# Two tokens across the partitions in the gate scatter of an expert layer: one L for a pair of tokens, an R with zeros, two products per pair, five row buffers

## Chip, cores and metric

The kernel runs on one core of a Trainium2 chip. The metric is device time in microseconds of one execution. The kernel before takes 1112.83 us, the median of three runs (1112.5 to 1113.57). A profiled execution, taken separately, has its own time.

## What is computed

The output is the sum of three things over 2048 tokens of 512 values: the input, a Fourier mixing of its layer norm (matrix products with given DFT matrices), and a product-key expert layer (PEER). The last is what the change touches:

```python
q = einsum("nd,dhc->nhc", xf, w_q)              # 32 heads
s1, s2 = q1 @ k1.T, q2 @ k2.T                   # 64 + 64 key scores per head
# the best two of each, their four sums, the best two of those:
top_s, top_e = ...                              # per token 32 heads x 2 experts out of 4096
g   = softmax(top_s, axis=-1)
act = gelu(einsum("nd,nhkd->nhk", xf, u[top_e]))
out = einsum("nhk,nhk,nhkd->nd", g, act, v[top_e])
```

Each token so has 64 entries, each an expert number and a gate.

## The kernel before

**Stages.** First comes a stage of some 440 us: layer norm, the Fourier part and, in 8 chunks of heads by 16 blocks of 128 tokens, the scores (`scores`, L793) and the choice of experts (`routing`, L630), whose lists go into `z`. Then comes the expert stage, on which the change bears. It does not gather rows of `u` and `v` for most tokens, but multiplies densely with all 4096 experts. For a block `b` of 128 tokens:

- `u_part(b, cg)` (L950), eight parts: 48 products of 128x128x128 per part give the scores of 512 experts (L959), and ScalarE evicts them through the gelu into `act` (L962).
- `g_mm(b, tg)` (L974), four groups of 32 tokens: makes the dense gate matrix G (4096 experts by 32 tokens) by products of one-hot matrices. An expert number is split as `e = 128*c + l`. For one token, `L[entry, l]` is 1 where `l` is the entry's low part and `R[entry, c]` is the gate where `c` is its high part; L transposed times R is that token's 128x32 table of gates. VectorE makes L by an equality (L983) and R by an equality and a product (L991, L994) from the compacted lists `cmp`; TensorE makes one 128x32 product per token (L996) into a PSUM tile `pg` of two banks, of which there are two.
- `w_part(b, tg)` (L1002): VectorE multiplies the table with the activations, in place in PSUM (L1007); ScalarE writes the float16 high half (L1012) and VectorE the rest (L1015), both into `act`. L1015 is the last reader of the `pg` tile.
- `v_part(b, pv, cg)` (L1019), eight parts of 12 products 128x128x512 (L1024), and `finish` (L1037).

**The entries.** A gate is kept as two float16 halves. Before the change the two halves are two entries with the same expert, so that a token has 128 entries, one in each partition: `z` has the rows low part, high part and gate, each of 2 experts x 2 halves x 32 heads. `compact` (L693) transposes the three rows of a block (L698) and copies them to `cmp` with each value doubled (L699).

**The last two blocks** (256 tokens, `NS`) go another way: `fetch` (L1046) gathers, with an indirect DMA issued by GpSimd, one row of `[u|v]` for each of 128 token partitions into one of `BUFS` = 6 row buffers (tag `ga`); `dot` (L1054) takes the product with x on VectorE (L1066); `gain` (L1069) scales the row on ScalarE (L1076, L1077, L1079); GpSimd adds it (L1084) and then issues the next fetch. There are 128 such rows. `paced` and `pick` spread these and a series of checks of the inputs (`cx`, `fit`) over the parts.

**The order.** The parts alternate: `v_part` of block b with `g_mm(b+1, 2)` after part 3 and `g_mm(b+1, 3)` after part 7, then `u_part` of block b+2 with `g_mm(b+2, 0)` and `g_mm(b+2, 1)` at the same places. A scheduler sets the final order on each engine; each engine then works strictly in its order, and semaphores make it wait.

L has two buffers and a group uses both, one for each 16 tokens; R has two buffers and a group uses one.

Of the kernel before, what the change touches and what calls it, by code (L numbers as in the profile page):

```python
# [10 lines left out]
F16 = mybir.dt.float16  # L11
# [4 lines left out]
AF = mybir.ActivationFunctionType  # L16
ALU = mybir.AluOpType
AX = mybir.AxisListType

P = 128  # L20
# [3 lines left out]
NT = S // P  # L24
H = 32
# [3 lines left out]
NC = E // P  # L29
# [7 lines left out]
def tile_fnet_peer(ctx, tc, x, ca, cb, c5, wt, wf, wr, wq, kt, ut, vn, uv, out):  # L37
# [14 lines left out]
    z_d = dram.tile([NT, P, 3 * P], F16, name="z_d")  # L52
# [189 lines left out]
    cmp_p = stE.enter_context(tc.tile_pool(name="cmpp", bufs=1, side="right"))  # L242
# [313 lines left out]
    def part_b(safe, stS, stP, stE, xt, u_sb, cmp_p):  # L556
# [54 lines left out]
        sp = stS2.enter_context(tc.tile_pool(name="sp", bufs=1, side="left"))  # L611
        z = sp.tile([P, NT, 3, 2, 2, H], F16, name="z")
# [17 lines left out]
        def routing(part, j, vals, idx, t0=0, t1=NT, ge=nc.gpsimd):  # L630
# [6 lines left out]
            hs = slice(j * HC, (j + 1) * HC)  # L637
            n = t1 - t0
            idx = idx[:, t0:t1]
            zi = z[:, t0:t1]  # L640
            c00, c01, c10, pm, i2s = t("c00"), t("c01"), t("c10"), t("pm"), t("i2s")
            if part == 0:
                a = vals[:, t0:t1, 0].rearrange("p i k h -> p i h k")
                b = vals[:, t0:t1, 1].rearrange("p i k h -> p i h k")
# [6 lines left out]
            elif part == 1:  # L651
                ex, g = c10, sp.tile([P, n, 2, HC], F32, tag="g", name=f"g{j}_{t0}", bufs=1)
# [4 lines left out]
                nc.vector.tensor_copy(zi[:, :, 2, :, 0, hs], g)  # L657
                if not safe and t1 == NT:
                    nc.gpsimd.tensor_copy(gts[:, :, :, hs], g[:, n - NS:])
                nc.vector.tensor_tensor(zi[:, :, 2, :, 1, hs], g, zi[:, :, 2, :, 0, hs], op=ALU.subtract)  # L660
            else:
# [31 lines left out]
        def compact(b, src, pool, tag):  # L693

            cmp = pool.tile([P, 3, P, 2], F16, tag=tag, name=f"cmp{b}")
            p = pc(f"zt{b}", F16) if b < 2 else psum.tile([P, 512], F16, tag="pb", name=f"zt{b}", bufs=2)
            for w in range(3):
                nc.tensor.transpose(p[:, w * P:(w + 1) * P], src[:, w], ident16)  # L698
            nc.scalar.activation(cmp, p[:, :3 * P].rearrange("p (w n) -> p w n", w=3).unsqueeze(3)  # L699
                                 .to_broadcast([P, 3, P, 2]), AF.Copy)  # L700
            CMP[b] = cmp
# [163 lines left out]
        for j in range(NCH):  # L865
# [8 lines left out]
            for i in range(NT):  # L874
# [20 lines left out]
                if j + 1 == NCH and i == NT - 1:  # L895
                    for b in range(2):
                        compact(b, z[:, b].rearrange("p w k t h -> p w (k t h)"), cmp_p, f"cmp{b}")
                    nc.sync.dma_start(z_d[2:4].rearrange("i p f -> p i f"),
                                      z[:, 2:4].rearrange("p i a k t h -> p i (a k t h)"))
# [6 lines left out]
        for part in range(3):  # L906
            routing(part, *pend, 4, NT, nc.vector)
        nc.sync.dma_start(z_d[4:].rearrange("i p f -> p i f"),
                          z[:, 4:].rearrange("p i a k t h -> p i (a k t h)"))
# [7 lines left out]
        RS = [lr.tile([P, 32, NC], F16, name=f"R{k}") for k in range(2)]  # L917
# [16 lines left out]
        BUFS = 6  # L934
# [10 lines left out]
        def compact_d(b):  # L945
            zb = bp.tile([P, 3, P], F16, tag="zb", name=f"zb{b}", bufs=1)
            nc.sync.dma_start(zb.rearrange("p a r -> p (a r)"), z_d[b])
            compact(b, zb, cmp_p, f"cmp{b % 2}")
# [25 lines left out]
        def g_mm(b, tg, after=None):  # L974
            cmp = CMP[b]
            p = pg(f"g{b}_{tg}")
            def bc(w, t0, t1, n):
                return cmp[:, w, tg * TG + t0:tg * TG + t1, :].unsqueeze(2).to_broadcast([P, t1 - t0, n // 2, 2])

            for hf in range(2):  # L980
                LS.append(LS.pop(0))
                L = LS[-1]
                nc.vector.tensor_tensor(  # L983
                    L.rearrange("p t (l two) -> p t l two", two=2),
                    io_lam.rearrange("p (l two) -> p l two", two=2).unsqueeze(1).to_broadcast([P, 16, P // 2, 2]),
                    bc(0, hf * 16, hf * 16 + 16, P), op=ALU.is_equal)
                if hf == 0:
                    RS.append(RS.pop(0))
                    R = RS[-1]
                    Rv = R.rearrange("p t (c two) -> p t c two", two=2)  # L990
                    nc.vector.tensor_tensor(  # L991
                        Rv, io_c.rearrange("p (c two) -> p c two", two=2).unsqueeze(1)
                        .to_broadcast([P, TG, NC // 2, 2]), bc(1, 0, TG, NC), op=ALU.is_equal)
                    nc.vector.tensor_tensor(Rv, Rv, bc(2, 0, TG, NC), op=ALU.mult)  # L994
                for t in range(16):
                    i = nc.tensor.matmul(p[:, hf, t * NC:(t + 1) * NC], L[:, t, :], R[:, hf * 16 + t, :],  # L996
                                         start=True, stop=True)
# [495 lines left out]
```

## Time and profile before

| | |
|---|---|
| time, median of three runs | 1112.83 us |
| the profiled execution: its time | 1110.31 us |
| its span, first to last instruction | 1108.5 us |
| mean granted TensorE clock | 0.988 |
| PE busy (matmul) | 1070.5 us, 97% |
| DVE (VectorE) busy | 963.9 us, 87% |
| ACT (ScalarE) busy | 717.3 us, 65% |
| POOL (GpSimd) busy | 595.4 us, 54% |
| DMA moved | 196.78 MB, 178 GB/s |

PE is TensorE's matmul row, PEld its loads of weights. In a row of the timeline the first number is the start in us, the second the busy time; `[...]` at its end is idle time ahead of it and what ended that. Matmuls overlap: the time between two starts is what one costs, and is less than the duration of one. "x" counts instructions.

### The profile page before, as it was taken

The numbers are of one execution on the slowest core, as the hardware profiler recorded it, in microseconds if no ns is written. First come the engines' busy times: TensorE is split into PE (matmuls) and PEld (weight loads), VectorE is DVE, ScalarE is ACT, GpSimd is POOL, SyncE is SP. The second block draws the span as 40 slices with busy tenths as digits, with TensorE's granted clock in tenths as the row PEclk, the third lists the DMA queues.
The fourth block names the chain that finished last, engine by engine and source line by source line (L and its number), as shares of the span: only waits on it lengthen the run. The fifth ranks groups of instructions, "written<-read, shape, count | busy, mean of one in ns | idle before, by whom it ended". The sixth has DMA issues, their size and how long they took to land. (4 is left out here: it accounts for less than half of the span.)

```text
span 1108.5 us, 28483 instructions
## 1 busy us (share of the span) xinstructions
PE 1070.5 (97%) x11070; PEld 696.6 (63%) x11070; DVE 963.9 (87%) x2748; ACT 717.3 (65%) x1326; POOL 595.4 (54%) x553
## 2 busy tenths in 40 slices
PE   5899999999999999999989999999999999999987
PEld 4355555454544544987675967858667696776933
DVE  6879897979999999987999798999998889998971
ACT  3566657778788767533756766668666776767650
POOL 0013537588797846211646575665575656556431
PEclk9799999999999999999999999999999999999999
DMA  8248153435445331463568667766876667666511
GB/s 326 84 168 288 39 210 99 174 130 208 152 153 197 110 123 65 152 212 92 183 189 248 193 206 244 223 220 191 242 232 214 209 204 252 222 200 200 166 29 51
DMA packets 84936, 196.78 MB, mean 178 GB/s; under 512 B 10770, under 2 KB 27559, under 8 KB 84792
## 3 DMA queue, kind: packets, MB, share of 16 engines
q1 hardware_dynamic: 63898, 123.55, 33.0%
q0 software_dynamic: 20736, 71.31, 21.7%
q8 instruction: 88, 1.44, 0.5%
q14 instruction: 56, 0.46, 0.1%
q10 hardware_dynamic: 158, 0.01, 0.0%
HBM read 177.74 MB, written 17.10 MB: 176 GB/s over the span
## 5 line engine op out<-in xcount | busy, mean ns | idle before, releaser
L799 PE MATMUL s<-m,xq 128*128 128x512 f16 x1536 | 338.9, 379 | 0.0
L959 PE MATMUL z<-xb,u 128*128 128x128 f16 x5376 | 306.4, 220 | 0.0
L959 PEld LDWEIGHTS <-u 128*128 128x128 f16 x5376 | 302.1, 98 | 0.0
L1024 PE MATMUL v<-v,act 128*128 128x512 f16 x1344 | 300.2, 382 | 1.6 <-DVE act L1015 1.6
L1084 POOL TENSOR_TENSOR ov<-ov,ga 128x512 f32<-128x512 f32 x128 | 176.9, 1382 | 206.9 <-ACT ga L1079 173.4
L799 PEld LDWEIGHTS <-xq 128*128 128x128 f16 x1536 | 148.3, 98 | 171.3 <-issue 0.2
L1024 PEld LDWEIGHTS <-act 128*128 128x128 f16 x1344 | 129.6, 98 | 153.2 <-issue 4.5
L983 DVE TENSOR_TENSOR L<-io_lam,cmp 128x2048 f16<-128x2048 f16 x112 | 154.7, 1405 | 31.2 <-PE g L996 31.1
L1050 POOL DMA_INDIRECT ga<-in_uv_dram,eix x128 | 153.4, 1198 | 48.1 <-POOL ov L1084 36.9
L807 DVE MAX8 vals<-ss 128x8 f32<-128x64 f32 x1024 | 152.5, 216 | 14.0 <-ACT ss L804 14.0
L962 ACT ACTIVATE act<-z,scl 128x512 f32<-128x512 f32 x112 | 76.1, 681 | 93.6 <-PE z L959 92.9
L811 DVE FIND_INDEX8 idx<-vals,ss 128x8 uint16<-128x256 f32 x256 | 107.1, 419 | 0.0
L804 ACT ACTIVATE ss<-s,wsc 128x512 f32<-128x512 f32 x112 | 75.5, 680 | 43.1 <-PE s L799 33.8
L1079 ACT ACTIVATE ga<-ga,za 128x512 f32<-128x512 f32 x128 | 92.3, 722 | 10.2 <-ACT za L1077 0.4
L781 ACT ACTIVATE cx<-cx 128x896 f32<-128x896 f32 x64 | 60.6, 947 | 48.7 <-DVE cx L761 36.3
L1066 DVE SCALAR_TENSOR_TENSOR ga<-ga,px 128x512 f32<-128x512 f32 x128 | 85.7, 676 | 0.2
L1012 ACT ACTIVATE act<-g 128x1024 f16<-128x1024 f32 x56 | 73.2, 1308 | 18.2 <-DVE g L1007 18.2
L1007 DVE SCALAR_TENSOR_TENSOR g<-act,scl,g 128x1024 f32<-128x1024 f32 x56 | 71.6, 1279 | 10.7 <-ACT act L962 6.6
L1015 DVE TENSOR_TENSOR act<-g,act 128x1024 f16<-128x1024 f32 x56 | 72.7, 1298 | 6.6 <-ACT act L1012 6.5
L169 POOL TENSOR_TENSOR wq<-wq,wh 128x1024 f16<-128x1024 f32 x26 | 55.5, 2136 | 24.2 <-ACT wq L166 23.7
L996 PE MATMUL g<-R,L 128*128 128x32 f16 x1792 | 53.8, 176 | 13.0 <-DVE act L1015 12.5
L996 PEld LDWEIGHTS <-L 128*128 128x128 f16 x1792 | 51.6, 96 | 21.7 <-DVE act L1015 8.7
(281 smaller groups left out, 1298.4 us busy)
## 6 DMA issues: line engine op xcount, KB each, us to landing
cx<-in_cb_dram SPq DMA_DIRECT2D x50, 448.0 KB
wq<-in_wq_dram SPq DMA_DIRECT2D x32, 512.0 KB
fit<-in_wq_dram SPq DMA_DIRECT2D x28, 512.0 KB
uv<-in_ut_dram SPq DMA_DIRECT2D x16, 512.0 KB
uv<-in_vn_dram SPq DMA_DIRECT2D x16, 512.0 KB
cx<-in_cb_dram SPq DMA_DIRECT2D x28, 224.0 KB
xq<-in_x_dram SPq DMA_DIRECT2D x8, 512.0 KB
xt_d<-xq SPq DMA_DIRECT2D x16, 256.0 KB
```

What stands on the lines that cost most here:

```text
L799: mm = nc.tensor.matmul(ps, xt[i][:, l, kd, :], m[:, r, kd, :], start=(n == 0), stop=(n == 3 * KD - 1))
L807: nc.vector.max(vals[:, i, w, :, h], s[:, g, :])
L811: nc.vector.max_index(idx[:, i, w].rearrange("p k h -> p (k h)"), vals[:, i, w, 0:2].rearrange("p k h -> p (k h)"), s[:, w * HC:g + 1, :]. ...
L959: mm = nc.tensor.matmul(p[:, cc * P:(cc + 1) * P], ug[:, l, c % 2, kd, :], xb[:, r, kd, :], start=(n == 0), stop=(n == 3 * KD - 1))
L962: GL[mm.ins.name] = nc.scalar.activation(act[:, cg * 4:cg * 4 + 4, :].rearrange("p c n -> p (c n)"), p, AF.Gelu_apprx_tanh, scale=zsc)
L983: nc.vector.tensor_tensor(L.rearrange("p t (l two) -> p t l two", two=2), io_lam.rearrange("p (l two) -> p l two", two=2).unsqueeze(1).to_ ...
L996: i = nc.tensor.matmul(p[:, hf, t * NC:(t + 1) * NC], L[:, t, :], R[:, hf * 16 + t, :], start=True, stop=True)
L1024: mm = nc.tensor.matmul(pv, w16[:, c, :, l], vg[:, r, c % 2, :], start=(c == 0 and k == 0), stop=(c == NC - 1 and k == 2))
L1050: nc.gpsimd.indirect_dma_start(out=t, out_offset=None, in_=uv, in_offset=bass.IndirectOffsetOnAxis(ap=eix[:, n].rearrange("p k h -> p (k h ...
L1066: nc.vector.scalar_tensor_tensor(t, t, 1.0, T["x"], op0=ALU.mult, op1=ALU.mult, accum_out=T["z", n][:, s:s + 1])
L1079: nc.scalar.activation(t, t, AF.Copy, scale=z)
L1084: T["a"] = nc.gpsimd.tensor_tensor(o, o, t, op=ALU.add)
```

## The change

The two halves of a gate are no longer two entries. `z` has five rows of 64 entries: low part, high part, gate high half, gate low half, and the low part once more. `compact` transposes two neighbouring rows at a time, four transposes, so that partitions 0 to 63 get one row and 64 to 127 the next; three copies then put the entries of even tokens in partitions 0 to 63 and those of odd tokens in 64 to 127 of `cmp`, now `[128, 4, 64 pairs, 2]`.

In `g_mm` one L of 16 x 128 columns serves the 16 pairs of a group. R has, for each half of the gate and each pair, 64 columns: 32 for the even token, filled in partitions 0 to 63, and 32 for the odd one, filled in partitions 64 to 127. The other quarters stay zero; GpSimd zeroes both R once. VectorE makes a one-hot matrix for the high parts once and multiplies it with the gates in four pieces of 64 partitions. A pair takes two products of 128x64, for the two halves of the gate, which add up in PSUM, both with the same L. There are so still 32 products in a group.

R takes twice the space, and there is a tile `one_hot`; `BUFS` goes from 6 to 5.

```diff
-    z = sp.tile([P, NT, 3, 2, 2, H], F16, name="z")
+    z = sp.tile([P, NT, 5, 2, H], F16, name="z")
...
-                for l in range(2):
-                    for w, v in enumerate((lc, e)):
-                        ge.tensor_copy(zi[:, :, w, :, l, hs], v)
+                for w, v in ((0, lc), (1, e), (4, lc)):
+                    ge.tensor_copy(zi[:, :, w, :, hs], v)
...
-            cmp = pool.tile([P, 3, P, 2], F16, tag=tag, name=f"cmp{b}")
+            cmp = pool.tile([P, 4, 64, 2], F16, tag=tag, name=f"cmp{b}")
...
-            for w in range(3):
-                nc.tensor.transpose(p[:, w * P:(w + 1) * P], src[:, w], ident16)
-            nc.scalar.activation(cmp, p[:, :3 * P].rearrange("p (w n) -> p w n", w=3).unsqueeze(3)
-                                 .to_broadcast([P, 3, P, 2]), AF.Copy)
+            for w in range(4):
+                nc.tensor.transpose(p[:, w * P:(w + 1) * P], src[:, w:w + 2].rearrange("p w s -> p (w s)"), ident16)
+            for a, w0, w1, o in ((0, 0, 4, 0), (1, 0, 3, 1), (1, 3, 4, -3)):
+                r = slice(64 * a, 64 * a + 64)
+                nc.scalar.activation(cmp[r, w0 + o:w1 + o], p.rearrange("p (w n a) -> p w a n", w=4, a=2)[r, w0:w1, a]
+                                     .unsqueeze(3).to_broadcast([64, w1 - w0, 64, 2]), AF.Copy)
...
-        RS = [lr.tile([P, 32, NC], F16, name=f"R{k}") for k in range(2)]
+        RS = [lr.tile([P, 2, 16, 2, NC], F16, name=f"R{k}") for k in range(2)]
+        one_hot = lr.tile([P, 16, NC], F16, name="one_hot")
+        for R in RS:
+            nc.gpsimd.memset(R, 0.0)
...
-        BUFS = 6
+        BUFS = 5
...
-            for hf in range(2):
-                LS.append(LS.pop(0))
-                L = LS[-1]
-                nc.vector.tensor_tensor(
-                    L.rearrange("p t (l two) -> p t l two", two=2),
-                    io_lam.rearrange("p (l two) -> p l two", two=2).unsqueeze(1).to_broadcast([P, 16, P // 2, 2]),
-                    bc(0, hf * 16, hf * 16 + 16, P), op=ALU.is_equal)
-                if hf == 0:
-                    RS.append(RS.pop(0))
-                    R = RS[-1]
-                    Rv = R.rearrange("p t (c two) -> p t c two", two=2)
-                    nc.vector.tensor_tensor(
-                        Rv, io_c.rearrange("p (c two) -> p c two", two=2).unsqueeze(1)
-                        .to_broadcast([P, TG, NC // 2, 2]), bc(1, 0, TG, NC), op=ALU.is_equal)
-                    nc.vector.tensor_tensor(Rv, Rv, bc(2, 0, TG, NC), op=ALU.mult)
-                for t in range(16):
-                    i = nc.tensor.matmul(p[:, hf, t * NC:(t + 1) * NC], L[:, t, :], R[:, hf * 16 + t, :],
-                                         start=True, stop=True)
+            LS.append(LS.pop(0))
+            RS.append(RS.pop(0))
+            L, R = LS[-1], RS[-1]
+            nc.vector.tensor_tensor(
+                two(L), io_lam.rearrange("p (l two) -> p l two", two=2).unsqueeze(1).to_broadcast([P, 16, P // 2, 2]),
+                bc(0, P), op=ALU.is_equal)
+            nc.vector.tensor_tensor(
+                two(one_hot), io_c.rearrange("p (c two) -> p c two", two=2).unsqueeze(1)
+                .to_broadcast([P, 16, NC // 2, 2]), bc(1, NC), op=ALU.is_equal)
+            for l in range(2):
+                for a in range(2):
+                    r = slice(64 * a, 64 * a + 64)
+                    nc.vector.tensor_tensor(two(R[r, l, :, a]), two(one_hot[r]), bc(2 + l, NC, r), op=ALU.mult)
+            pv = p.rearrange("p h n -> p (h n)")
+            for t in range(16):
+                for l in range(2):
+                    i = nc.tensor.matmul(pv[:, t * 64:(t + 1) * 64], L[:, t, :],
+                                         R[:, l, t].rearrange("p a c -> p (a c)"), start=l == 0, stop=l == 1)
```

In the changed kernel the lines of the expert stage stand 8 lines later: L is made at L991, the one-hot at L994, R at L1000, the products at L1004, and L1007, L1015, L1039 and L1066 of before are L1015, L1023, L1047 and L1074.

**Where the order moves.** On TensorE, where a gate group late in the expert stage starts behind a `v_part` (v is its product, g the `pg` tile, L and R the one-hot matrices). Before:

```order
L1024 LDWEIGHTS act_13340
L1024 MATMUL v_14787<-v_5189,act_13340 128x512
L996 LDWEIGHTS L_5792
L996 MATMUL g_2_14859<-R_5794,L_5792 128x32
L996 LDWEIGHTS L_5792
L996 MATMUL g_2_14859<-R_5794,L_5792 128x32
```

and now:

```order
L1032 LDWEIGHTS act_13440
L1032 MATMUL v_14907<-v_5183,act_13440 128x512
L1004 LDWEIGHTS L_5789
L1004 MATMUL g_2_14979<-R_5791,L_5789 128x64
L1004 LDWEIGHTS L_5789
L1004 MATMUL g_2_14979<-R_5791,L_5789 128x64
```

Every product still has its load of weights, also the second of a pair with the same L; the product is 64 columns wide and no longer 32.

On VectorE, from the end of a `v_part` (the row of y) to the L1015 of before that frees a `pg` tile. L_5792 and L_5793 are the two buffers of L, R_5794 and R_5795 those of R. Before:

```order
L1039 SCALAR_TENSOR_TENSOR y_14934<-v_14787,scl,y_14934 128x512
L983 TENSOR_TENSOR L_5792<-io_lam,cmp_14926 128x2048
L983 TENSOR_TENSOR L_5793<-io_lam,cmp_14926 128x2048
L1007 SCALAR_TENSOR_TENSOR g_3_14994<-act_14130,scl,g_3_14994 128x32x32
L991 TENSOR_TENSOR R_5795<-io_c,cmp_14926 128x1024
L994 TENSOR_TENSOR R_5795<-R_5795,cmp_14926 128x1024
L1066 SCALAR_TENSOR_TENSOR ga_45_14845,za_11802<-ga_45_14845,px_11801 128x512
L1015 TENSOR_TENSOR act_14130<-g_2_14859,act_14130 128x32x32
```

and now (L_5789 and L_5790 are the two buffers of L, R_5791 and R_5792 those of R):

```order
L1047 SCALAR_TENSOR_TENSOR y_15059<-v_14907,scl,y_15059 128x512
L1000 TENSOR_TENSOR R_5792<-one_hot,cmp_15048 64x16x32
L1015 SCALAR_TENSOR_TENSOR g_3_15119<-act_14241,scl,g_3_15119 128x32x32
L991 TENSOR_TENSOR L_5790<-io_lam,cmp_15048 128x2048
L1000 TENSOR_TENSOR R_5792<-one_hot,cmp_15048 64x16x32 x3
L994 TENSOR_TENSOR one_hot<-io_c,cmp_15048 128x512
L1074 SCALAR_TENSOR_TENSOR ga_45_15028,za_11883<-ga_45_15028,px_11882 128x512
L1023 TENSOR_TENSOR act_14241<-g_2_14979,act_14241 128x32x32
```

A group writes one L and not both; the product with the activations has moved ahead of L; the one-hot of the next group stands ahead of the row that frees the `pg` tile.

On GpSimd, around the fetch of row 50 of the first gathered block (ga is a row buffer, ov the sum of the rows). Before:

```order
L1084 TENSOR_TENSOR ov_11920<-ov_11920,ga_43_14785 128x512
L1050 DMA ga_49_15092<-in_uv_dram,eix 128x1024
L1084 TENSOR_TENSOR ov_11920<-ov_11920,ga_44_14808 128x512
L1050 DMA ga_50_15154<-in_uv_dram,eix 128x1024
L1084 TENSOR_TENSOR ov_11920<-ov_11920,ga_45_14845 128x512
```

and now:

```order
L1092 TENSOR_TENSOR ov_12003<-ov_12003,ga_44_14965 128x512
L1058 DMA ga_49_15281<-in_uv_dram,eix 128x1024
L1092 TENSOR_TENSOR ov_12003<-ov_12003,ga_45_15028 128x512
L1058 DMA ga_50_15432<-in_uv_dram,eix 128x1024
L1092 TENSOR_TENSOR ov_12003<-ov_12003,ga_46_15084 128x512
```

Row 50 is fetched after the add of row 45 and no longer after that of row 44.

More of the change, by code (lines that the diff above doesn't have):

```diff
@@ new lines, in bc, with two @@
+            def bc(w, n, r=slice(0, P)):
+                v = cmp[r, w, tg * 16:tg * 16 + 16, :]
+                return v.unsqueeze(2).to_broadcast([v.shape[0], 16, n // 2, 2])
+            def two(v):
+                return v.rearrange("p t (c two) -> p t c two", two=2)
+            LS.append(LS.pop(0))
[4 more added lines that the diff above has]
+                bc(0, P), op=ALU.is_equal)
```

16 lines of the change are left out of this document (7 added, 9 removed).

## The prediction

> **What bounds the kernel now.** I read the busy shares first, then the expert stage alone, then who waits for whom there.
>
> ```profile
> PE 1070.5 (97%) x11070; PEld 696.6 (63%) x11070; DVE 963.9 (87%) x2748; ACT 717.3 (65%) x1326; POOL 595.4 (54%) x553
> 475.00:1055.00 580.00, 571.28 (x7700) 430.17 (x7697) 522.39 (x739) 381.71 (x805) 328.69 (x260) 0.99 0.67 205
> ```
>
> The second row is the stretch of the expert stage: 580 us, in which TensorE is busy for 571.28 and VectorE, the third sum, for 522.39, which is 90%. TensorE sets the time; what it loses, it loses by waiting.
>
> ```profile
> PE g L996 <- DVE act L1015: 12.5, 8, 3.9
> PE v L1024 <- DVE act L1015: 1.6, 1, 1.6
> DVE L L983 <- PE g L996: 29.7, 19, 4.6
> ```
>
> TensorE's waits in this stage sum to 14.1 us, all ended by L1015. The gate products wait for the `pg` tile that L1015 reads last, two groups back. VectorE in turn waits 29.7 us for TensorE before it may write L. The two hold each other.
>
> ```profile
> 540.00:580.00 40.00, 36.91 (x448) 26.96 (x447) 38.97 (x55) 22.96 (x48) 23.51 (x19) 0.96 0.63 186
> 820.00:860.00 40.00, 40.00 (x483) 28.13 (x482) 36.25 (x52) 25.46 (x54) 23.23 (x19) 0.97 0.70 222
> ```
>
> Behind two of the waits the granted clock dips: 0.96 and 0.97 of 40 us are 1.6 and 1.2 us lost beside the waits. So some 17 us at most can be won back from VectorE being late. One of these waits in the timeline, TensorE first (with two later waits), then ScalarE, VectorE and GpSimd:
>
> ```profile
> 804.70 0.95 PE L996 MATMUL g<-R,L 128*128 128x32 f16 x32
> 805.50 10.88 PE L959 MATMUL z<-xb,u 128*128 128x128 f16 x192
> 818.07 0.95 PE L996 MATMUL g<-R,L 128*128 128x32 f16 x32 [1.68 <-DVE act L1015]
> ...
> 1063.68 0.95 PE L996 MATMUL g<-R,L 128*128 128x32 f16 x32 [3.92 <-DVE act L1015]
> 1081.46 20.46 PE L1024 MATMUL v<-v,act 128*128 128x512 f16 x94 [1.60 <-DVE act L1015]
> ```
> ```profile
> 810.20 1.30 ACT L1012 ACTIVATE act<-g 128x1024 f16<-128x1024 f32 x1
> ```
> ```profile
> 805.29 1.81 DVE L983 TENSOR_TENSOR L<-io_lam,cmp 128x2048 f16<-128x2048 f16 x1 [0.93 <-PE g L996]
> ...
> 810.04 1.21 DVE L983 TENSOR_TENSOR L<-io_lam,cmp 128x2048 f16<-128x2048 f16 x1
> ...
> 813.07 2.40 DVE L991 TENSOR_TENSOR R<-io_c,cmp 128x1024 f16<-128x1024 f16 x1
> ...
> 816.72 1.29 DVE L1015 TENSOR_TENSOR act<-g,act 128x1024 f16<-128x1024 f32 x1
> ```
> ```profile
> 813.63 1.28 POOL L1084 TENSOR_TENSOR ov<-ov,ga 128x512 f32<-128x512 f32 x1
> ```
>
> ScalarE has done its half at 811.50. VectorE takes L1015 at 816.72 only, since it waited 0.93 us for an L buffer until the burst at 804.70 was under way, then built two Ls and an R, one of them stretched to 2.40 us while GpSimd's add ran. L1015 ends at 818.01 and TensorE goes on at 818.07.
>
> **TensorE, part by part.** The number of gate products stays 56 x 32 = 1792; each gets 64 columns for 32.
>
> ```profile
> 140.34 0.22 PE L147 MATMUL m<-sums,wh 128*128 128x64 f16 x2
> ...
> 141.04 2.75 PE L799 MATMUL s<-m,xq 128*128 128x512 f16 x12
> ```
>
> At 32 columns a burst takes 805.50 - 804.70 = 0.80 us by the rows above, 25 ns per product. The kernel has products of just the new form in its first stage, L147: 64 columns, f16, an own load of weights each, three adding up in the same place. 24 of them run from 140.34 to 141.04, 29 ns each. So +4 ns x 1792 = **+7.1 us**, all on TensorE's path. The fourth transpose of a block costs one product of 128 columns, (10.88 - 0.22)/191 = 56 ns by the row at 805.50; 14 blocks give **+0.8 us**. Of the price of a narrow product the Trainium skill says otherwise (TensorE: Matmul & The Clock Gate, section Back-to-back issue gap): its table has about 60 cycles, an issue floor of about 25 ns, for anything from 1 to 64 columns. By that the wider product would be free and the sum 7 us lower; the trace agrees with it at 32 columns and not at 64, where L147 shows 29 ns, so the row decides.
>
> **VectorE, per group.** Alone, by the shortest and middle durations, and with what GpSimd's adds cost them, by the means:
>
> ```profile
> L983 DVE TENSOR_TENSOR L<-io_lam,cmp x112: 1148/1216/2979, 449.2 to 1067.7; 128x2048 f16<-128x2048 f16 x112
> L991 DVE TENSOR_TENSOR R<-io_c,cmp x56: 666/682/2493, 452.6 to 1063.5; 128x1024 f16<-128x1024 f16 x56
> L994 DVE TENSOR_TENSOR R<-R,cmp x56: 617/692/2186, 453.9 to 1066.6; 128x1024 f16<-128x1024 f16 x56
> ...
> L983 DVE TENSOR_TENSOR L<-io_lam,cmp 128x2048 f16<-128x2048 f16 x104 | 145.2, 1420 | 29.8 <-PE g L996 29.7
> L991 DVE TENSOR_TENSOR R<-io_c,cmp 128x1024 f16<-128x1024 f16 x51 | 49.4, 970 | 1.1 <-ACT cmp L699 1.0
> L994 DVE TENSOR_TENSOR R<-R,cmp 128x1024 f16<-128x1024 f16 x51 | 45.3, 889 | 1.2
> ```
>
> Before, alone: 2 x 1.22 + 0.68 + 0.69 = 3.81 us; as it ran, by busy time: 145.2/52 + 49.4/51 + 45.3/51 = 4.65 us. So being blocked costs 0.84 us per group. Now there is one L and five operations of 512 elements. No row has that size. A line through 1024 (0.68) and 2048 elements (1.22) gives 0.54 per 1024 and 0.14 fixed, so 0.41 us each; the upper bound is the 0.69 of 1024 elements, if 64 partitions and short pieces earned nothing. Alone that is 1.22 + 5 x 0.41 = 3.27 us, or 4.67 at the upper bound. I take the line, as the operations differ in length alone. How the blocking scales is open: by time, 0.84 x 3.27/3.81 = 0.72, so 3.99 per group; by operation, 0.84/4 x 6 = 1.26, so 4.53. I take the first, as the row at 813.07 waited once, for one add. The Trainium skill has that as a lock (SBUF — State Buffer, section SBUF: two separate sides): a VectorE operation with two inputs in SBUF and a GpSimd one that reads SBUF exclude each other for a whole instruction. By that it is the 128 adds that count, not the number of pieces; the trace agrees at 813.07. So VectorE gets 0.66 us per group back, some 34 us in 52 groups. The other end, 0.69 us each and blocked by operation, is 4.67 + 1.26 = 5.93 us, a loss of 1.3 per group.
>
> The **waits for L** matter as much. Both L buffers were taken by each group, so that L of the next could not be begun before the burst; now a group takes one, and the 29.7 us should mostly go. What is late next is L1015 for want of ScalarE's half: between 811.50 and the burst's due time, 805.50 + 10.88 = 816.38, there are 4.9 us, of which L1015 takes 1.3.
>
> At 818.07, VectorE saves 0.93 of the wait and an L of 1.2 at 810.04; with the R pieces that covers the 1.68. The longest, 3.9 us at 1063.68, comes before the last block, whose groups 2 and 3 follow each other after two parts of v and not four; I expect half of it to stay. The 1.6 us on L1024 before 1081.46 is the last group's, whose L1015 stands behind the y of the block before: that stays. Of the 14.1 us I take 9.5 as gone, and 2.5 us of clock with it: **-12.0 us**. Bounds: 17 gone, and below nothing: at the loss of 1.3 us in 52 groups VectorE would need 522 + 67 = 589 of the 580 us and take some 9 us more.
>
> **Costed at nothing.** ScalarE's copies into `cmp`:
>
> ```profile
> L699 ACT ACTIVATE cmp<-zt 128x768 f16<-128x768 f16 x12 | 9.7, 806 | 37.7 <-PE zt L698 37.7
> L962 ACT ACTIVATE act<-z,scl 128x512 f32<-128x512 f32 x100 | 68.1, 681 | 81.1 <-PE z L959 80.4 <-issue 0.7
> L783 ACT ACTIVATE cx<-cx 128x128 f32<-128x128 f32 x36 | 10.8, 299 | 0.0
> ```
>
> One of 0.81 becomes three, by the rows of 512 and 128 elements some 0.68 + 0.55 + 0.30 = 1.53 us. ScalarE's idle time, 580 - 382 us, hides 0.7 x 14 = 10 us; uncovered, it delays the L1012 queued behind it once per block, 12 x 0.7 = 8 us.
>
> ```profile
> 455.57 0.24 POOL L659 COPY gts<-g 128x16 f32<-128x16 f32 x1 [12.88 <-DVE g L656]
> L1114 POOL MEMSET cx_r<- 128x1024 f32 x1 | 1.0, 966 | 0.0
> ```
>
> The zeroing of R, two of 1 to 2 us (1024 elements take 0.97), falls into GpSimd's 12.88 idle us before 455.57; R is first written at 453.9. If it started late, the first gate burst would wait those 2 to 4 us, once. The cast less per chunk on GpSimd and the smaller `z` touch nothing that TensorE waits for.
>
> Row buffers:
>
> ```profile
> L1050 POOL DMA_INDIRECT ga<-in_uv_dram,eix x123: 950/1102/1853, 490.2 to 1054.9; - x123
> L1066 DVE SCALAR_TENSOR_TENSOR ga<-ga,px x128: 660/675/693, 518.8 to 1075.1; 128x512 f32<-128x512 f32 x128
> DMA to landing us min/median/max: 4.1/5.1/8.1
> ```
>
> A row is used every 556/128 = 4.35 us, so six buffers are 26 us for a row's cycle and five 21.7. Dot, add (1.3 by the row at 813.63), issue and landing take 0.7 + 1.3 + 1.1 + 5.1 = 8.2 us, so 13.5 are left for the scaling on ScalarE and for queues. That hides it; uncovered, a late row holds VectorE's queue up, L1015 with it.
>
> **Sum.** On the profiled execution, 1110.3 us (span 1108.5 and 1.8 around it): 1110.3 + 7.1 + 0.8 - 12.0 = 1106.2. The median of the timed runs lies 2.5 us above that execution, so **1108.7 us**.
>
> **Rivals.** *VectorE stays late* (20%): the pieces are blocked one by one and run at the 1024-element price, so that VectorE wins nothing, and L1015 keeps its place behind them. It decides from a group that costs the 4.65 us of now: with 3.27 us alone that is 1.38 us of blocking, 0.23 per operation, and as much is had by pieces of 0.69 us. TensorE then pays 7.9 us and gets nothing: 1112.8 + 7.9 = 1120.7 us, slower, and 9 us more at the far end. For it: two more operations per group, all of the kind that GpSimd's adds block. Against it: the waits for L go anyway. *Late rows* (12%): the five buffers make VectorE wait at L1074. If a row in every third block lands at the longest instead of the median time, 3 us late, and the slack of L1015 covers 2 of them, four blocks lose 1 us each: 1112.7, no change. For it: the distance of dots varies, and the lead shrinks by 4.35 us. Against it: 13.5 us in hand. *All waits go* (11%): L is ready so early that 17 us come back: 1112.8 + 7.9 - 17 = 1103.7. Against it: the waits at the end have causes that stay. *The wider product is free* (2%): the 25 ns of a product of 32 columns are a floor that 64 columns do not pass, so 7.1 us less: 1101.6. Against it: L147 at 29 ns. (The table of the Trainium skill's page TensorE: Matmul & The Clock Gate, as above, speaks for it.) *The change doesn't do what it says* at the loads: the products of a pair share L, yet each keeps its load, so nothing is won there; this is in the sum.
>
> **Chances.** The forecast has 55%. Two runs differ by about 0.2% without cause, 2.2 us here: below 1110.6 is faster, above 1115.1 slower. Of the 55, 44 are faster and 11 the same; the 11 and the 2 are faster; of the 12, 9 the same and 3 slower; the 20 are slower. Faster 0.57, same 0.20, slower 0.23. The likeliest case alone ranges from 1104 to 1113. To leave out 2 in 10, the range goes to 1101 below and 1119 above.
>
> **What would show it.** L1004 at 29 ns from start to start, a burst of 0.93 us. L1000 at 0.41 us alone and not 0.69, with a mean below 0.6. DVE L <- PE g under 5 us. PE g <- DVE L1023 under 5 us in all, the dips at 560 and 820 gone. No wait of L1074 on a DMA over 1 us. The forecast is wrong if TensorE's waits stay over 10 us, or if the gate products find a new wait, on R's last piece or on GpSimd's zeroing.

## The result and the profile after

The changed kernel takes 1123.91 us, the median of 4 runs (1121.8 to 1126.07), beside 1112.66 us for the kernel before in 4 runs of the same chip. The ratio is 1.0114 with a 95% interval of 1.0094 to 1.0133: slower, where 1108.7 us was forecast, and above the range's 1119 us. The two medians alone are 11.3 us apart, a ratio of 1.0101; figures below go by the 1.0114. The profiled execution took 1126.07 us, its span is 1124.2 us, 15.7 us more than before, at a granted clock of 0.986 (0.988 before).

The page's first row, and the stretch of the expert stage that the prediction showed (TensorE, its loads, VectorE, ScalarE, GpSimd):

```profile
PE 1081.6 (96%) x11084; PEld 706.3 (63%) x11084; DVE 944.6 (84%) x2858; ACT 724.3 (64%) x1354; POOL 582.8 (52%) x548
```
```profile
475.00:1055.00 580.00, 567.96 (x7546) 429.03 (x7544) 497.62 (x818) 379.40 (x811) 309.12 (x255) 0.99 0.68 202
```

VectorE did become lighter: 497.62 of 580 us, not 522.39. Yet TensorE, which sets the time, got through 7546 products in that stretch and not 7700. Who waits for whom, from 475 us to the end, TensorE first, then VectorE (total us, times, longest):

```profile
PE g L1004 <- DVE act L1023: 17.9, 12, 4.2
PE v L1032 <- DVE act L1023: 1.6, 1, 1.6
```
```profile
DVE g L1015 <- ACT act L966: 26.5, 9, 4.3
DVE one_hot L994 <- ACT cmp L700: 21.6, 11, 3.4
...
DVE R L1000 <- PE g L1004: 12.9, 10, 5.6
DVE y L1047 <- PE v L1032: 11.5, 3, 5.7
DVE g L1015 <- PE g L1004: 9.1, 7, 5.3
DVE act L1023 <- ACT act L1020: 9.0, 10, 2.9
```

The 29.7 us of waits for L are no longer there. In their place stand 21.6 us in which one_hot waits for `cmp` (new), 26.5 us in which the product with the activations, now L1015, waits for the gelu (6.6 before) and 12.9 us for R. TensorE's waits, ended by L1023 (before: L1015), rose from 14.1 to 19.5 us.

I also use a count of **lost time**: over all gate products, the time from the start of the product before to its own start, less the usual spacing of that product. It takes in what the waits leave out, such as pauses inside a group's products. It is 14.6 us before and 20.3 after. With it the 15.7 us add up, all from starts of products: the first u product starts at 445.2 and not 443.2 us (2.0, ahead of the stage), the products themselves cost 7.9 more (gate products 45.1 to 52.2 at 25.1 and 29.1 ns from start to start, transposes 0.8), and the lost time is 5.7 more: 15.6.

### The profile page after: what moved, and what is told of

It is laid out like the page before. It is cut to its first block, busy times and chain, and to the rows that moved or that the text cites. A ratio compares the mean times of both kernels' runs of the same rounds, so it can differ in the third digit from the quotient of the medians.

```text
span 1124.2 us, 28682 instructions
## 1 busy us (share of the span) xinstructions
PE 1081.6 (96%) x11084; PEld 706.3 (63%) x11084; DVE 944.6 (84%) x2858; ACT 724.3 (64%) x1354; POOL 582.8 (52%) x548
## 5 line engine op out<-in xcount | busy, mean ns | idle before, releaser
L1092 POOL TENSOR_TENSOR ov<-ov,ga 128x512 f32<-128x512 f32 x128 | 174.4, 1362 | 233.1 <-ACT ga L1087 176.3
L1058 POOL DMA_INDIRECT ga<-in_uv_dram,eix x128 | 141.1, 1102 | 48.2 <-POOL ov L1092 35.6
L1000 DVE TENSOR_TENSOR R<-one_hot,cmp 64x512 f16<-64x512 f16 x224 | 133.3, 595 | 16.3 <-PE g L1004 13.4
L1015 DVE SCALAR_TENSOR_TENSOR g<-act,scl,g 128x1024 f32<-128x1024 f32 x56 | 71.1, 1282 | 36.0 <-ACT act L966 26.5
L1074 DVE SCALAR_TENSOR_TENSOR ga<-ga,px 128x512 f32<-128x512 f32 x128 | 86.1, 678 | 0.5
L1023 DVE TENSOR_TENSOR act<-g,act 128x1024 f16<-128x1024 f32 x56 | 72.7, 1298 | 9.4 <-ACT act L1020 9.2
L1004 PE MATMUL g<-R,L 128*128 128x64 f16 x1792 | 61.2, 193 | 18.1 <-DVE act L1023 17.9
L1004 PEld LDWEIGHTS <-L 128*128 128x128 f16 x1792 | 58.7, 98 | 26.2 <-issue 20.4
L991 DVE TENSOR_TENSOR L<-io_lam,cmp 128x2048 f16<-128x2048 f16 x56 | 71.3, 1273 | 0.1
```

The source lines that it names most:

```text
L1000: nc.vector.tensor_tensor(two(R[r, l, :, a]), two(one_hot[r]), bc(2 + l, NC, r), op=ALU.mult)
L1004: i = nc.tensor.matmul(pv[:, t * 64:(t + 1) * 64], L[:, t, :], R[:, l, t].rearrange("p a c -> p (a c)"), start=l == 0, stop=l == 1)
L1058: nc.gpsimd.indirect_dma_start(out=t, out_offset=None, in_=uv, in_offset=bass.IndirectOffsetOnAxis(ap=eix[:, n].rearrange("p k h -> p (k h ...
L1074: nc.vector.scalar_tensor_tensor(t, t, 1.0, T["x"], op0=ALU.mult, op1=ALU.mult, accum_out=T["z", n][:, s:s + 1])
L1092: T["a"] = nc.gpsimd.tensor_tensor(o, o, t, op=ALU.add)
```

## The experiments

Each ran in five rounds beside the kernel before on its chip. Chips and hours differ by up to 4 us (the kernel before: 1109.6 to 1113.4), so ratios are compared; a microsecond figure for a ratio is that ratio times 1112.7. "Waits" are TensorE's before gate products. Waits and lost time come from one profiled execution of each kernel, the ratios from all its runs.

| run | ratio to before (95%) | waits, us | lost time, us |
|---|---|---|---|
| before | 1 | 12.5 | 14.6 |
| the change | 1.0114 (1.0094 to 1.0133) | 17.9 | 20.3 |
| e1 five row buffers | 0.9999 (0.9983 to 1.0015) | 11.7 | 13.6 |
| e2 wide products | 1.0023 (1.0004 to 1.0043) | 9.7 | 11.5 |
| e3 three L | 0.9975 (0.9962 to 0.9989) | 9.6 | 11.7 |
| e9 short multiplication | 0.9933 (0.9911 to 0.9954) | 6.8 | 7.3 |
| e6 before, short adds | 0.9839 (0.9820 to 0.9858) | 0.7 | 2.2 |
| e5 change, short adds | 0.9948 (0.9931 to 0.9966) | 2.8 | 3.2 |
| e13 change, one copy | 1.0127 (1.0108 to 1.0146) | 16.1 | 18.2 |
| e7 change, one_hot 3 steps ahead | 1.0060 (1.0037 to 1.0083) | 11.0 | 13.3 |
| e8 as e7, and L1015 held | 1.0061 (1.0040 to 1.0082) | 13.4 | 16.7 |
| e14 L1015 held alone | 1.0092 (1.0065 to 1.0118) | 17.3 | 19.6 |
| e11 change, one_hot 5 steps ahead | 1.0011 (0.9997 to 1.0026) | 8.7 | 10.0 |
| e12 as e11, and L with it | 1.0004 (0.9987 to 1.0022) | 10.1 | 11.5 |
| e15 as e12, and a later burst | 0.9969 (0.9953 to 0.9984) | 5.2 | 6.7 |
| e10 before, three L and a later burst | 0.9924 (0.9901 to 0.9946) | 8.0 | 9.9 |

### Parts of the change, put into the kernel before

**Row buffers alone.**

```diff
-        BUFS = 6
+        BUFS = 5
```

> The kernel before with five row buffers instead of six and nothing else. Theory (the row buffers are innocent: the changed kernel's dots waited 0.5 us in all): within 0.2% of 1112.7 us, TensorE's waits before the gate products unchanged at 12 to 15 us. Rival (late rows): at least 2.5 us slower, with waits of VectorE's dot line on a DMA of over 1 us.

Nothing moved: 0.9999. The rival falls.

**The wide product alone.**

```diff
-                    i = nc.tensor.matmul(p[:, hf, t * NC:(t + 1) * NC], L[:, t, :], R[:, hf * 16 + t, :],
+                    n = 2 if t < 15 else 1
+                    i = nc.tensor.matmul(p[:, hf, t * NC:(t + n) * NC], L[:, t, :],
+                                         R[:, hf * 16 + t:hf * 16 + t + n, :].rearrange("p t c -> p (t c)"),
                                          start=True, stop=True)
```

> The kernel before with gate products of 64 columns for 32 (product t also writes the columns of token t+1, which the next product overwrites; the last of a half stays at 32), so 1680 of the 1792 products are wide and VectorE's work is the old. Theory (TensorE pays 4 ns for each wide product and gets nothing back): +6.7 us, 1119.4 us, with the group's products at 29 ns from start to start and TensorE's waits on VectorE unchanged at 12 to 16 us. Rival 1 (a product of 32 or 64 columns costs the same): 1112.7 us. Rival 2 (a longer burst gives VectorE time, so part of the price comes back out of the waits): 1115 to 1117 us with waits of 8 to 10 us.

The price is there: 29 ns from start to start (29.6 as a mean, with 42 products at 50 to 54 ns). But the kernel got only 2.6 us slower (0.4 to 4.8), as the second rival had it:

```profile
PE g L997 <- DVE act L1017: 9.7, 6, 4.1
```

TensorE's own longer work gives VectorE time, and 2.8 of the 12.5 us of waits go. Here, where the two engines wait for each other, a term on one was not paid in full.

**L's waits alone.** The kernel before with a third L in the room of a row buffer.

```diff
-        LS = [lr.tile([P, 16, P], F16, name=f"L{k}") for k in range(2)]
+        LS = [lr.tile([P, 16, P], F16, name=f"L{k}") for k in range(3)]
...
-        BUFS = 6
+        BUFS = 5
```

> The kernel before with three L buffers for two, in the room of the sixth row buffer; VectorE's and TensorE's work is the old. The theory on record (the waits for L make L1015 late): the 29.7 us of VectorE's waits for L fall below 10 and TensorE's waits of 12.5 us fall by half or more with them, 1100 to 1107 us. Rival (VectorE's strict order: idle time that is taken from one wait comes back in another, and L1015 ends no earlier): the waits for L fall, TensorE's waits stay over 10 us, 1111 to 1115 us.

```profile
DVE L L983 <- PE g L996: 20.8, 12, 4.4
```
```profile
PE g L996 <- DVE act L1015: 9.6, 6, 4.0
```

Neither expectation was met in full. A third of L's waits for TensorE went (4.5 us in which L waits for `cmp` are new), and the kernel won 2.8 us (0.25%), a quarter of what the prediction hung on them at the most.

**A lighter VectorE alone.**

```diff
-                    nc.vector.tensor_tensor(Rv, Rv, bc(2, 0, TG, NC), op=ALU.mult)
+                    nc.vector.tensor_tensor(Rv[:, 0:2], Rv[:, 0:2], bc(2, 0, 2, NC), op=ALU.mult)
```

> The kernel before with the multiplication of R by the gates on 2 of 32 tokens (the gates of the other 30 are left out), so that VectorE alone gets lighter, by some 0.6 us in each group, more than the change gave it (0.45 us); TensorE's work is the old. The reasoning on record (a lighter VectorE brings L1015 forward and with it the gate products): at least 6 us faster, a ratio of 0.990 to 0.995, TensorE's waits below 7 us. Rival (time freed on VectorE turns into waits in its strict order): a ratio of 0.997 to 1.001, with waits for L, y and gelu longer by what was freed.

By groups, with the mean behind the comma:

```profile
L994 DVE TENSOR_TENSOR R<-R,cmp 128x64 f16<-128x64 f16 x51 | 20.6, 404 | 1.2
```

45.3 us became 20.6, and the kernel 7.5 us faster. So the reasoning on record holds in the old order: some 25 us less for VectorE are worth 7 us of TensorE's lost time (14.6 to 7.3). The change took about as much from VectorE (22 us, below), and those 7 us did not come. What follows looks for them.

### GpSimd's adds

The sum of the rows is cut to 16 of 512 columns, in both kernels.

```diff
-                T["a"] = nc.gpsimd.tensor_tensor(o, o, t, op=ALU.add)
+                T["a"] = nc.gpsimd.tensor_tensor(o[:, 0:16], o[:, 0:16], t[:, 0:16], op=ALU.add)
```

> The changed kernel with GpSimd's adds of the row path on 16 of 512 columns (the sum of the other columns is left out), so that its short pieces are hardly blocked any more. Rival (the pieces are blocked one by one and this keeps L1023 late): L1000's mean falls from 0.60 to about 0.42 us, TensorE's lost time before gate products from 20 us to 8 to 12, 1112 to 1116 us on the scale of 1112.7 before. Theory (the order's waits for cmp and gelu make L1023 late, not the blocking): the pieces get shorter, the lost time stays at 15 us or more, 1118 to 1122 us.

> The kernel before with GpSimd's adds of the row path on 16 of 512 columns (the sum of the other columns is left out), beside the changed kernel with the same (0.9948 of the kernel before). Theory (with no blocking neither kernel keeps TensorE waiting, and what is left between the two is TensorE's price alone): 0.987 to 0.990, that is 5 to 8.5 us under the changed kernel with short adds. Rival (the blocking hurts the changed kernel's six pieces more than the four operations before): 0.993 or more, no more than 2 us under it.

In the changed kernel with short adds, R's pieces by groups and the wait that is left on TensorE:

```profile
L1000 DVE TENSOR_TENSOR R<-one_hot,cmp 64x512 f16<-64x512 f16 x206 | 86.5, 420 | 31.5 <-PE g L1004 29.1
```
```profile
PE g L1004 <- DVE act L1023: 2.8, 1, 2.8
PE v L1032 <- DVE act L1023: 1.6, 1, 1.6
```

In the first of these runs the rival was right, and by more than it said: without the blocking the changed kernel wins 18 us (1.0114 to 0.9948), although one_hot still waits 22.1 us for `cmp` and L1015 31.9 us for the gelu. Such waits at the head of VectorE's order thus cost TensorE little by themselves (its lost time is 3.2 us); they do harm when VectorE has no time left. The kernel before wins the same from short adds (0.9839, 18 us), so the blocking explains the level of both kernels, not the difference. With it gone the difference is 12.1 us, more than the 5 to 8.5 expected. Some 7.8 are the products; in the two profiled executions 2.1 lie in the wait ahead of the last block (3.0 against 0.9) and 4.0 in pauses of 0.2 to 0.6 us between u products, for which the profile names no cause. That last part stays open.

### ScalarE's copies

```diff
-            for a, w0, w1, o in ((0, 0, 4, 0), (1, 0, 3, 1), (1, 3, 4, -3)):
-                r = slice(64 * a, 64 * a + 64)
-                nc.scalar.activation(cmp[r, w0 + o:w1 + o], p.rearrange("p (w n a) -> p w a n", w=4, a=2)[r, w0:w1, a]
-                                     .unsqueeze(3).to_broadcast([64, w1 - w0, 64, 2]), AF.Copy)
+            nc.scalar.activation(cmp, p.rearrange("p (w n a) -> p w a n", w=4, a=2)[:, :, 0]
+                                 .unsqueeze(3).to_broadcast([P, 4, 64, 2]), AF.Copy)
```

> The changed kernel with one ScalarE copy into cmp for three (the second token's half and the arrangement of the rows are left out, so the gates are wrong), 0.7 us less on ScalarE in each block. Theory (ScalarE's copies cost nothing): a ratio of 1.009 to 1.014 as the change itself. Rival (the copies delay ScalarE's halves and cmp, and these keep one_hot and L1023 waiting): 1.000 to 1.005, VectorE's wait for cmp falls from 21.6 below 10 us.

1.0127, as slow as the change. The copies are innocent.

### The order on VectorE

Where does L1023 stand? A wait of the changed kernel on the timeline, VectorE first, then ScalarE, GpSimd and TensorE:

```profile
564.26 0.42 DVE L994 TENSOR_TENSOR one_hot<-io_c,cmp 128x512 f16<-128x512 f16 x1
564.72 1.72 DVE L1000 TENSOR_TENSOR R<-one_hot,cmp 64x512 f16<-64x512 f16 x4
566.48 0.43 DVE L994 TENSOR_TENSOR one_hot<-io_c,cmp 128x512 f16<-128x512 f16 x1
...
568.95 1.28 DVE L1015 SCALAR_TENSOR_TENSOR g<-act,scl,g 128x1024 f32<-128x1024 f32 x1
...
570.35 1.22 DVE L991 TENSOR_TENSOR L<-io_lam,cmp 128x2048 f16<-128x2048 f16 x1
571.48 1.71 DVE L1000 TENSOR_TENSOR R<-one_hot,cmp 64x512 f16<-64x512 f16 x4
573.23 1.42 DVE L994 TENSOR_TENSOR one_hot<-io_c,cmp 128x512 f16<-128x512 f16 x1
...
575.18 1.28 DVE L1023 TENSOR_TENSOR act<-g,act 128x1024 f16<-128x1024 f32 x1
```
```profile
568.60 1.30 ACT L1020 ACTIVATE act<-g 128x1024 f16<-128x1024 f32 x1
```
```profile
573.10 1.26 POOL L1092 TENSOR_TENSOR ov<-ov,ga 128x512 f32<-128x512 f32 x1 [0.70 <-ACT ga L1087]
```
```profile
562.91 10.88 PE L963 MATMUL z<-xb,u 128*128 128x128 f16 x192
576.51 1.09 PE L1004 MATMUL g<-R,L 128*128 128x64 f16 x32 [2.71 <-DVE act L1023]
```

ScalarE's half is ready at 569.90. VectorE starts L1023 at 575.18, since an L, four pieces of R and a third one_hot, stretched to 1.42 us while the add at 573.10 runs, come ahead: between two bursts it makes two sets of R and the one_hot of a third. The gates are ready long before they are used; the burst is held up by the tile that L1023 must free. In the order quoted ahead of the prediction that can be seen: the one_hot of the next group stands ahead of L1023. Over the 53 L1023 between 480 and 1100 us, the time from the end of ScalarE's half to their start has a mean of 2.48 us before and 2.65 after. A lighter VectorE brought it forward by nothing.

The order can be counted too. I take the rows that free a tile in 50 of the 56 groups (the fourth to the fifty-third), and what stands ahead of each for a later group than that of the burst that waits for it. Before, that is the equality of R in 39 of the 50, and never an L. Now it is an L in 49, a one_hot in 48 and a second one_hot, for one group further on, in 24.

So I held the scheduler back, with no work added or removed: one_hot may be placed only behind the product group that lies LEAD steps of the program before its burst (a step is a `u_part` or `v_part` of some 2.6 us).

```diff
+        MM = []
+        LEAD = 3
...
-            nc.vector.tensor_tensor(
+            i = nc.vector.tensor_tensor(
                 two(one_hot), io_c.rearrange("p (c two) -> p c two", two=2).unsqueeze(1)
                 .to_broadcast([P, 16, NC // 2, 2]), bc(1, NC), op=ALU.is_equal)
+            if len(MM) > LEAD:
+                follow(i.ins, MM[-1 - LEAD])
...
                 mm = v_part(b, pv, cg)
+                MM.append(mm)
...
                 mm = u_part(b + 2, cg)
+                MM.append(mm)
```

> The changed kernel with the scheduler held from placing one_hot ahead of the product group three steps before its own burst; no work is added or removed. Theory (one_hot of the next block, placed ahead of the L1023 of this one, waits 21.6 us for ScalarE's cmp and makes L1023 late): that wait falls below 5 us, TensorE's lost time before gate products falls from 20.3 to about 15 us, 1118 to 1120 us. Rival (the stalls come from elsewhere, such as the waits of the line after it for gelu, 26.5 us, and GpSimd's adds): the wait goes and the time stays within 1122 to 1126 us.

6.0 us came back (1.0114 to 1.0060), as expected in size; no wait of one_hot for `cmp` is left. But three steps are too few:

```profile
PE g L1008 <- DVE act L1027: 8.2, 8, 2.8
PE g L1008 <- DVE R L1004: 2.8, 4, 1.1
```

Next, L1015 held as well, behind the step after which the program has it.

```diff
-            nc.vector.scalar_tensor_tensor(w, act[:, :, ts], fw, w, op0=ALU.mult, op1=ALU.mult)
+            i = nc.vector.scalar_tensor_tensor(w, act[:, :, ts], fw, w, op0=ALU.mult, op1=ALU.mult)
+            if MM:
+                follow(i.ins, MM[-1])
```

> The changed kernel with one_hot held back as in the run before (1.0060 of the kernel before) and L1015 too, which the scheduler may no longer place ahead of the v or u group after which it stands in the program. Theory (what is left of VectorE's time is lost at the heads of its order, 30.5 us for gelu alone): the wait for gelu falls below 15 us, TensorE's lost time before gate products from 13.3 to 8 to 10 us, a ratio of 1.001 to 1.003. Rival (the wait for gelu is time in which nothing late stands behind it): a ratio of 1.005 to 1.007.

The wait for the gelu went, the time stayed (1.0061): the rival was right, and the bursts now waited 9.8 us for R. Then one_hot further ahead, and L with it (`j` is the instruction that makes L):

```diff
-        LEAD = 3
+        LEAD = 5
```
```diff
+                follow(j.ins, MM[-1 - LEAD])
```

> The changed kernel with one_hot held back to five steps before its burst and not three, since at three (1.0060) the bursts waited 2.8 us for R's pieces and paused inside for 3.4. Theory (a good place for the gate operations lies between; the order costs what is left): no pauses inside bursts, TensorE's lost time before gate products 8 to 10 us, a ratio of 1.001 to 1.004. Rival (earlier than three steps the head of the order waits again, as in the change): 1.006 to 1.010.

> As the one with one_hot held back to five steps before its burst, and L held back with it, so that no operation of a group's gates can be placed ahead of work that is due sooner. Theory (what stands ahead of L1023 decides): a ratio of 1.000 to 1.003. Rival (L, with two buffers, is never in the way): the same ratio as with one_hot alone, within 0.002.

1.0011 and 1.0004: 11.5 and 12.2 us of the 12.7 us are back, by the order alone (with the intervals of these ratios, within some 3 us), and no pause inside a burst is left. L adds nothing that can be told from none. In the first of the two, 49 of the 50 rows that free the tile (L1027 there) still have a later group's L ahead, but only 2 a later one_hot: it is one_hot, and R behind it, whose place counts. TensorE's waits with one_hot five steps ahead, and with L too:

```profile
PE g L1008 <- DVE act L1027: 8.7, 4, 4.0
```
```profile
PE g L1009 <- DVE act L1028: 10.1, 6, 3.9
```

The same place as above on VectorE, ScalarE and TensorE, with L and one_hot five steps ahead:

```profile
564.12 1.22 DVE L993 TENSOR_TENSOR L<-io_lam,cmp 128x2048 f16<-128x2048 f16 x1
565.26 0.42 DVE L996 TENSOR_TENSOR one_hot<-io_c,cmp 128x512 f16<-128x512 f16 x1
565.71 1.83 DVE L1005 TENSOR_TENSOR R<-one_hot,cmp 64x512 f16<-64x512 f16 x2
...
570.37 1.39 DVE L1005 TENSOR_TENSOR R<-one_hot,cmp 64x512 f16<-64x512 f16 x1
571.79 1.29 DVE L1020 SCALAR_TENSOR_TENSOR g<-act,scl,g 128x1024 f32<-128x1024 f32 x1
...
573.73 1.31 DVE L1028 TENSOR_TENSOR act<-g,act 128x1024 f16<-128x1024 f32 x1
```
```profile
569.91 1.30 ACT L1025 ACTIVATE act<-g 128x1024 f16<-128x1024 f32 x1
```
```profile
564.23 10.88 PE L965 MATMUL z<-xb,u 128*128 128x128 f16 x192
575.09 1.09 PE L1009 MATMUL g<-R,L 128*128 128x64 f16 x32
```

One group's gates and not two stand ahead of the row that frees the tile, L1028 here; it ends at 575.04, and the burst does not wait. The mean time from ScalarE's half to that row fell from 2.65 to 1.64 us. That mean alone proves little: it is 0.72 us in the run below, where L1015, and ScalarE's half with it, comes later and TensorE waits as long as ever. The hold was not tried on the kernel before, which has R of a later group ahead of L1015 too, so what the same hold would win there is open.

In these two runs the wait for the gelu fell as well. To tell the two placements apart, L1015 alone was held (the second diff of this part without the first's lines on one_hot):

> The changed kernel with L1015 alone held back to its place in the program; one_hot and L stay where the scheduler puts them. Theory (one_hot ahead of L1023 is the harm, the wait for gelu has nothing late behind it): the wait for gelu goes, the ratio stays at 1.008 or more. Rival (the wait for gelu is the harm): 1.000 to 1.004, as with the gates held back five steps.

```profile
PE g L1005 <- DVE act L1026: 17.3, 12, 4.5
```
```profile
DVE one_hot L995 <- ACT cmp L700: 24.8, 8, 5.8
```

1.0092, and no wait for the gelu: the gates' place decides, not L1015's.

### Versions that beat the kernel before

In the last two blocks the third group's burst stands one step later. First with the kernel before and three L, then with the changed kernel and its gates held back.

```diff
-                vw, vg = {0: 0, 2: 1, 4: 2, 6: 3}, {2: 2, 4: 3}
+                vw, vg = {0: 0, 2: 1, 4: 2, 6: 3}, {3: 2, 4: 3}
```

> The kernel before with three L buffers and five row buffers (ratio 0.9975 in the run before), and in the last two blocks the gate products of the third group one step later (after the fourth v step, not the third), since TensorE waits 4.2 us before them. Theory (that wait is the distance between the group's two ends, not VectorE's load): it falls to 1 to 2 us and 2 to 3 us are won, a ratio of 0.994 to 0.996. Rival (the wait moves to the next group or to the end of the block's last group): the ratio stays within 0.0015 of 0.9975.

> The changed kernel with L and one_hot held back five steps (ratio 1.0004) and, as in the faster version of the kernel before, the gate products of the third group one step later in the last two blocks. Theory (the wait there is the distance in the program): the wait falls from 4.05 to about 2 us and the ratio to 0.997 to 0.999, still some 5 us behind that faster version (0.9924) since TensorE's 7.8 us are paid. Rival (with its lighter VectorE the changed kernel draws level): 0.991 to 0.994.

```profile
1060.58 0.95 PE L996 MATMUL g<-R,L 128*128 128x32 f16 x32 [2.09 <-DVE act L1015]
```
```profile
1066.44 1.09 PE L1009 MATMUL g<-R,L 128*128 128x64 f16 x32 [1.54 <-DVE act L1028]
```

The waits there fell from some 4 us to 2.09 and 1.54, so half of them or more was the distance in the program. The kernel before won more by it than the 2 to 3 us expected (0.9975 to 0.9924, 5.7 us), of which its lost time shows 1.8; the rest is not explained. The kernel before with three L, five row buffers and the later burst is the fastest here that computes everything, 1104.77 us beside 1112.51 (0.9924, 8.5 us by the ratio); the changed kernel so mended takes 1109.79 (0.9969, 3.4 us), 5 us behind it.

## Why the prediction was wrong

**TensorE's price, +7.1 and +0.8 us: right,** 7.1 and 0.8 us by the starts. R's product at 64 columns:

```profile
L1004 PE MATMUL g<-R,L x1792: 189/193/203, 458.6 to 1087.1; 128*128 128x64 f16 x200
```

The rival of the free wider product falls: the products start 29.1 ns apart, as L147's did. The Trainium skill's table (TensorE: Matmul & The Clock Gate, section Back-to-back issue gap), one value for 1 to 64 columns, agrees with the trace at 32 and not at 64.

**VectorE's group, 3.99 us: the piece alone right, the blocking not.** By groups from 480 to 1100 us, and the pieces alone:

```profile
L1000 DVE TENSOR_TENSOR R<-one_hot,cmp 64x512 f16<-64x512 f16 x206 | 125.8, 611 | 15.4 <-PE g L1004 12.9
...
L991 DVE TENSOR_TENSOR L<-io_lam,cmp 128x2048 f16<-128x2048 f16 x51 | 65.2, 1279 | 0.1
L994 DVE TENSOR_TENSOR one_hot<-io_c,cmp 128x512 f16<-128x512 f16 x51 | 26.5, 520 | 22.8 <-ACT cmp L700 21.6
```
```profile
L1000 DVE TENSOR_TENSOR R<-one_hot,cmp x224: 348/422/2082, 454.9 to 1078.7; 64x512 f16<-64x512 f16 x112
```

A piece alone takes 0.42 us, where 0.41 was worked out. By the means a group is 4 x 0.61 + 1.28 + 0.52 = 4.24 us, where it was 4.65: 0.41 us won and not 0.66, some 22 us in the stage and not 34. What the adds cost a group is the same as before: (611 - 422) x 206 + (1279 - 1213) x 51 + (520 - 425) x 51 = 47 us in 51 groups, 0.92 us each (medians from the view of a line), and by the rows of before 46 us. I took it to shrink with the time of the work, from 0.84 to 0.72. By the lock of the Trainium skill (SBUF — State Buffer, section SBUF: two separate sides) a VectorE operation with two inputs in SBUF and a GpSimd one that reads SBUF shut each other out for a whole instruction. From this the prediction drew that the adds count, not the pieces, and the 46 and 47 us agree; I then scaled by time all the same.

**The step that failed: TensorE's waits, -12.0 us.** It rested on two things: that the waits for L would go, and that a lighter VectorE would then reach L1015 (now L1023) sooner. The first came true and was worth little: 2.8 us for a third of these waits in the kernel before. The second holds in the old order, 7.5 us for a VectorE lighter by 25 us. In the new order it failed: L1023 comes no sooner behind ScalarE's half (2.65 us, 2.48 before), and TensorE's waits rose from 14.1 to 19.5 us. The prediction took the old order over and did not price the new one, in which the scheduler put gates of later groups, one_hot and R, ahead of the L1023 that the next burst waits for. Holding them back is worth 11.5 to 12.2 us. That the L buffer now left free gave the scheduler this freedom is not shown: with only one_hot held, the later L still stands ahead and costs nothing that can be seen. VectorE's freed time became waits for `cmp`, gelu and R; that these left it too little time behind them, where the adds then blocked it, fits the runs with short adds and is argued from them. With the gates five steps ahead the change comes to +0.4 to +1.2 us, where the prediction had -4.1. TensorE's price of 7.9 us is still in that; what offsets it is shown in part only, as the lost time of those two executions lies 3.1 to 4.6 us below that of before.

**Costed at nothing: right** for the row buffers (0.9999 alone; dots waited 0.5 us in all, landing has a median of 5.3 us and not 5.1) and for ScalarE's copies (1.0127 with one; worked out as 1.53 us, they take 0.59 + 0.49 + 0.26 = 1.33).

**The rivals.** *All waits go* fell with TensorE's waits. The time of *VectorE stays late*, 1120.7 us, came nearest, and its effect is the one seen: L1023 stays late and TensorE pays. Its mechanism was another: the pieces do not run at the price of 1024 elements and VectorE does win time. Of the signs named, these came true: 29 ns, the piece at 0.42 us with a mean of 0.595 over all 224, L's waits, no wait of the dots. L1023 failed with 17.9 us where under 5 was asked, the dips of the clock behind the waits only moved (to 578 and 830 us), and TensorE's waits of more than 10 us were what the text had named as making it wrong.

## What to carry to other kernels

Before counting on the time that an engine saves, read in the new order what now stands ahead of the row that the bounding engine waits for, and price it; here the order showed it and it was given no price. Preparation such as these gates can be tied to a number of steps ahead of its use: here three were too few, five left 0.4 to 1.2 us of the loss, and no limit left 12.7. Where two engines hold each other up, price an edit by putting it alone into the old kernel, since a gain on one engine or a loss on the other may be passed on only in part (7 us of longer products cost 2.6). And try a repair on the old kernel as well, which was left out here.

## What the runs showed of the hardware

What GpSimd's adds cost VectorE's gate operations did not change when these were cut differently: 46 us with four operations in a group and 47 with six shorter ones, both by means less medians. None can be seen once the adds are 0.31 us long and not 1.36 to 1.38 (the pieces of R have a mean of 0.420 us, with a median of 0.422 under long adds). Both kernels then gain 18 us, more than any edit of the gates. L1015 and L1023 of the changed kernel, with one input in PSUM, show no such stretching: their means are 1.28 and 1.30 us with long adds and with short ones.
